# A two-pass plan for engine order, fixed places for early attention, and results staged in dead x rooms (block attention and relu-squared FFN, one core)

## The chip, the cores and the metric

The kernel runs on one core of one Trainium2 chip. Its time is the device time of one execution in microseconds (us); the median of three runs is 923.54 us (923.27 to 924.87). A profile is one more execution, recorded by the hardware. PE is the matrix engine (PEld its weight loads), DVE the vector engine, ACT the scalar engine, POOL the general one, SP the engine that mostly issues DMA transfers.

## The reference

Inputs: q, k, v of shape (8 batches, 8 heads, 576 positions, 64) in float32, and two weight matrices of float64, `w_in` (512 x 2048) and `w_out` (2048 x 512).

```
scores = q_c @ k_c^T / 8           # inside chunks of 64 positions
attn   = exp(scores - max); attn /= (sum(attn) + 1e-9)
x      = attn @ v_c                # heads side by side: (4608, 512)
h      = x @ w_in
out    = relu(h)**2 @ w_out        # (4608, 512)
```

## The kernel before

**Blocks.** The 4608 rows are 36 pairs of chunks (128 rows each), in nine blocks of four pairs. A block's FFN takes 16 steps, one for each 128 of the 2048 hidden columns. Step f multiplies a slab of `w_in` with the block's x (twelve matmuls, line L606 in `mm_in`, into tile h), applies relu (L617), square (L621 on DVE or L623 on ACT), and splits the result into a high and a low part (gh on L630, gl on L633). Two steps later (`LAG`) twelve matmuls on L643 (`mm_out`) add it to four accumulators o, one for each pair. Each product is three matmuls (high x high, high x low, low x high), since a single fp32r part does not hold float32. In a list of PE operations the three count as one entry.

**Results.** After step 15 each accumulator is copied out (`keep`, L651; even pairs on ACT, odd ones on DVE) into one of two slots of a tile called stage, and stored from there (`store`, L656). The accumulators' banks are those that the next block's first L643 matmuls write.

**Weights.** They arrive as float64 (`fetch_w`, L155 and L157, 512 KB a slab) in a tile called raw, viewed as 32-bit words: word 0 is the low one, word 1 the high one. `convert_w` makes an fp32 value of the bits and splits it: ups (L169, ACT) takes the rounding bits from word 0; sign (L173, DVE) writes the sign and top exponent bit as half words; size (L179, ACT) is the absolute value of word 1; clamp (L183, DVE) bounds it; shift (L188, DVE) moves it by three bits into tile a; up (L192, DVE) adds the two; high (L197, ACT) and low (L208, DVE) give the two parts in tile w. There are 32 slabs (items), ordered i0, i1, i2, o0, i3, o1 and so on (i of `w_in`, o of `w_out`). The first six are converted one by one (`SINGLE = 6`), the others two at a time. Tile a lies, for every other group, in the room that is later the stage tile.

**Attention of the first two blocks** (`Pair`, lines L494 to L582) is done in float32 by whole pairs: q and k turned on PE (L494), copied (L505, L509), scores (L518), maximum, difference, exponential, sum, reciprocal, product (L526 to L544), probabilities turned (L555, L561), values (L569), x placed as high and low part (`place`, L580 and L582). Pairs 0 to 3 lead; nothing of the FFN can start before their x. Pairs 4 to 7 run during block 0. The raw q and k of all eight lie in rooms that the last eight weight slabs take over, so these slabs are fetched only when a pair has been turned. v goes to vbd (L286), q and k to qk_raw (L250).

**Later attention** (`Unit`, half the heads of a pair at a time, lines L303 to L453) is spread through the FFN of the block before, at written places (`SPOTS`, and `LEAD` for the first). Its q and k come to three ring tiles (L278), for pair 8 first to the stage tile, and are transposed on DVE (L308). PE computes scores on L355, turns probabilities on L402 and computes values on L428; POOL does the product with 1/sum (L394), v's low part (L345) and x's low part (L453).

**Order.** `Plan.add` collects operations with an engine, an estimated cost, and tokens read and written. `Plan.run` simulates the engines once, from the start: always the operation that can start first, then the one with the earlier due time (or a rank given by hand). The order so found is the order in which instructions are issued to each engine; SP takes its early loads in the written order. Engines run their queues strictly in order.

Of the kernel before, what the change touches and what calls it, by code (L numbers as in the profile page):

```python
# [21 lines left out]
def kernel(  # L22
# [40 lines left out]
    SINGLE = 6  # L63
    XV = 4
    FROM = (8, 12, 16, 24)
    V_FROM = (8, 12, 16, 24)
    RANK = (8, 12, 16, 20)
    blocks = [4] * 9
    LAG = 2
    GBUFS = 2  # L70
# [88 lines left out]
    def convert_w(g):  # L159
# [8 lines left out]
        def ups():  # L168
            nc.scalar.activation(word(0).bitcast(I32), word(0), AF.Copy, scale=2.0 ** -29)  # L169

        def sign():
            half = rooms_of[g, "raw"].bitcast(U16)
            nc.vector.tensor_scalar(  # L173
                half[:, :, :, 1], half[:, :, :, 3], 0x8000, 0x4000, op0=ALU.bitwise_and, op1=ALU.bitwise_or
            )

        def size():
            a = word(1).bitcast(F32)
            nc.scalar.activation(a, a, AF.Abs)  # L179

        def clamp():
            a = word(1).bitcast(F32)
            nc.vector.tensor_scalar(a, a, EXP_MIN, EXP_MAX, op0=ALU.max, op1=ALU.min)  # L183

        def shift():
            pool, tag = (gp, "o") if g % 2 else (wst, "a")
            st["a"] = a = pool.tile([P, 2, DM], U32, name=f"a{g}", tag=tag, bufs=1)[:, :k]
            nc.vector.tensor_scalar(a, word(1), 3, 0xFFFFFFF8, op0=ALU.logical_shift_left, op1=ALU.bitwise_and)  # L188

        def up():  # L190
            c = st["a"].bitcast(I32)
            nc.vector.tensor_tensor(c, c, word(0).bitcast(I32), op=ALU.add)  # L192
# [19 lines left out]
        return ups, sign, size, clamp, shift, up, high, low  # L212
# [76 lines left out]
    class Unit:  # L289
# [155 lines left out]
        def place(self, part):  # L445

            xh, xl = x_of(self.b)
            dst = (slice(None), slice(self.hq * HP, (self.hq + 1) * HP), slice(self.j * P, (self.j + 1) * P))
            src = self.x.rearrange("p a c i -> p a (c i)")
            if part == 0:  # L450
                nc.scalar.copy(xh[dst], src)  # L451
            else:
                nc.gpsimd.tensor_tensor(xl[dst], src, xh.bitcast(F32)[dst], op=ALU.subtract)  # L453

    def x_of(b):
        if b not in xt:
            n = XB[b % 2]
            xt[b] = tuple(
                xp.tile([P, NCC, n * P], F32R, name=f"x{m}{b}", tag=f"x{m}{b % 2}") for m in "hl"
            )  # L460
        return xt[b]
# [16 lines left out]
    class Pair:  # L478
# [95 lines left out]
        def place(self, part):  # L574
            b = block_of[self.u]
            j = self.u - first_pair[b]
            ps = self.xt.rearrange("p a c i -> p a (c i)")
            xh, xl = (x[:, :, j * P:(j + 1) * P] for x in x_of(b))
            if part == 0:
                nc.scalar.copy(xh, ps)  # L580
            else:
                nc.vector.tensor_tensor(xl, ps, xh.bitcast(F32), op=ALU.subtract)  # L582
# [7 lines left out]
    class Step:  # L590
# [7 lines left out]
        def mm_in(self, c, i):  # L598
            if c == 0 and i == 0:
# [3 lines left out]
            xh, xl = xt[self.b]  # L603
# [3 lines left out]
                self.h[:, :self.n], a[:, c], bb[:, c, :self.n],  # L607
# [40 lines left out]
        def keep(self, j, n):  # L648
            o = stage(n)
            copy = nc.vector.tensor_copy if j % 2 else nc.scalar.copy  # L650
            copy(o, acc[self.b, j])  # L651
            kept[self.b, j] = o
# [10 lines left out]

    ffn = [Step(b, f) for b, f in steps]
# [5 lines left out]
    class Plan:  # L670
# [35 lines left out]
        def run(self):  # L706
# [20 lines left out]
            while open_:  # L727
# [17 lines left out]
                for x in after[n]:  # L745
                    ready[x] = max(ready[x], end + self.hop(n, x))
                    waits[x] -= 1
                    if not waits[x]:
                        open_.add(x)
            assert len(order) == len(ops)  # L750
# [6 lines left out]
    def program():  # L757
# [19 lines left out]
        def fetch(n):  # L777
            where = []
            for m in together[group_of[n]] if not place_in[n] else ():
                u = m - (n_items - NN)  # L780
                where += [("q", u), ("k", u)]
                if 2 <= u + XV < lead:
                    where.append(("v", u + XV))
            add(SP, ISSUE, lambda: fetch_w(n), writes=[("raw", n), *where], size=P * DM * 8)
# [18 lines left out]

        def turns(u):
# [3 lines left out]
            add(PE, 4 * 0.11, lambda: x.turn(0), [("q", u), "ident"], [bq])  # L808
# [3 lines left out]
            add(PE, 4 * 0.11, lambda: x.turn(1), [("k", u), "ident"], [bk])  # L812
            add(ACT, ONE, x.keep_k, [bk], [("kt", i)])

        def scores(u):
# [4 lines left out]
            add(PE, 16 * 0.11 + w, x.scores, [("qbd", i, 0), ("qbd", i, 1), ("kt", i)], [bs])  # L820
# [9 lines left out]

        def values(u):
            x = prs[u]
            i = u % 2
            bp, bx = x.banks["pt"], x.banks["xt"]
            tt = "g" if x.lead and i else "tt"
            if x.lead and u:
                p.rank = 0.9 + (u - 1) / 10
            add(PE, 4 * 0.11, x.turn_p, [("e", i), "ident"], [bp])
            add(ACT, ONE, x.keep_p, [bp], [tt])
            if x.lead and u:  # L840
                p.rank = 1 + u / 10
            add(PE, 16 * 0.11, x.values, [("v", slot_of(u)), tt], [bx])
            place(u)

        def attention(u):
            banks(u)
            for stage in (turns, scores, shares, values):
                stage(u)
# [17 lines left out]
        def place(u):  # L866
            x = prs[u]
            bx = x.banks["xt"]
            add(ACT, ONE, lambda: x.place(0), [bx], [("xh", u, hq) for hq in range(NQ)])
            add(DVE, TWO, lambda: x.place(1), [bx] + [("xh", u, hq) for hq in range(NQ)], [("xl", u, hq) for hq in range(NQ)])  # L870

        def convert(n):
# [4 lines left out]
            ups, sign, size, clamp, shift, up, high, low = convert_w(g)  # L877
            a = ["a"] if g % 2 == 0 else [("ob", 0), ("ob", 1)]
            raw = [("raw", n) for n in ns]
            half, two, one = (HALF, TWO, ONE) if len(ns) == 1 else (TWO, TWO + 0.53, ONE + 0.37)  # L880
# [319 lines left out]
```

## Time and profile before

| | us |
|---|---|
| median of 3 runs | 923.54 |
| the profiled execution | 923.09 |
| its span, first to last instruction | 921.3 |
| PE busy | 906.7 (98%) |
| DVE busy | 688.7 (75%) |
| ACT busy | 640.1 (69%) |
| POOL busy | 209.9 (23%) |
| mean granted PE clock | 0.999 of full speed |

Busy times are sums over the span. Matmuls overlap in PE's pipeline: a record's length is more than the distance to the next one, so a full row of PE says that it was never empty, not that it ran at its best. In rows of the timeline the columns are start, duration, engine, line, operation, output<-input, shapes, count; in brackets at the end, how long the engine idled before it and what ended that.

### The profile page before, as it was taken

Reading aid. Unit: us, or ns where it says so; the run is one execution under the profiler, and the core shown is the slowest. Engines: PE = TensorE matmul, PEld = TensorE weight load, DVE = VectorE, ACT = ScalarE, POOL = GpSimd, SP = SyncE. Lnnn points to the kernel's source line nnn. Section 1 sums busy time; section 2 is a strip of 40 time slices with the busy share of each in tenths; the row PEclk is TensorE's granted clock in tenths of the full one; section 3 lists DMA queues with packets and bytes.
Section 4 is the critical chain, followed back from the end, with each engine's and each line's share of the span. In section 5 each row is a group of like instructions: output and inputs, shape, how many; then the busy total and the mean of one; then the engine's idle time right before and its main releaser. Section 6 shows DMA issues by size and latency. Waiting matters only on the chain. (4 is left out here: it accounts for less than half of the span.)

```text
span 921.3 us, 14689 instructions
## 1 busy us (share of the span) xinstructions
PE 906.7 (98%) x4402; PEld 752.3 (82%) x4402; DVE 688.7 (75%) x1499; ACT 640.1 (69%) x1443; POOL 209.9 (23%) x351
## 2 busy tenths in 40 slices
PE   8999999999999999999999999999999999999997
PEld 7778888888778888888888888888888888888886
DVE  5989987889887778777888878777877787742111
ACT  5878877887777777777777777777777777743232
POOL 2000003333333323333222223322233333300000
PEclk9999999999999999999999999999999999999999
DMA  8889106222232223222232232223322231001001
GB/s 181 266 221 292 46 15 135 51 52 49 64 72 44 43 45 90 49 43 39 74 54 47 47 81 50 44 47 67 72 45 43 43 90 36 1 1 47 0 1 46
DMA packets 222671, 62.85 MB, mean 68 GB/s; under 512 B 207744, under 2 KB 215936, under 8 KB 222592
## 3 DMA queue, kind: packets, MB, share of 16 engines
q1 hardware_dynamic: 220480, 61.39, 28.9%
q10 hardware_dynamic: 2112, 0.52, 0.3%
q8 instruction: 36, 0.59, 0.3%
q14 instruction: 43, 0.35, 0.1%
HBM read 52.43 MB, written 9.44 MB: 67 GB/s over the span
## 5 line engine op out<-in xcount | busy, mean ns | idle before, releaser
L606 PE MATMUL h<-xh,w 128*128 128x512 f32 x1152 | 402.4, 396 | 1.1 <-DVE w L208 0.7
L643 PE MATMUL o<-w,gh 128*128 128x512 f32 x1152 | 359.0, 393 | 2.7 <-DVE stage L651 2.4
L606 PEld LDWEIGHTS h<-xh,w 128*128 128x128 f32 x1152 | 216.1, 188 | 45.0 <-DVE w L208 3.0
L643 PEld LDWEIGHTS o<-w,gh 128*128 128x128 f32 x1152 | 211.3, 188 | 47.7 <-DVE stage L651 5.8
L606 PE MATMUL h<-xl,w 128*128 128x512 f32 x576 | 225.2, 391 | 0.4 <-POOL xl L453 0.4
L643 PE MATMUL o<-w,gl 128*128 128x512 f32 x576 | 224.3, 389 | 0.0
L633 DVE TENSOR_TENSOR gl<-g,gh 128x512 fp32r<-128x512 f32 x144 | 103.3, 718 | 106.5 <-ACT gh L630 99.8
L617 ACT ACTIVATE g<-h 128x512 f32<-128x512 f32 x144 | 86.0, 597 | 86.1 <-PE h L606 72.8
L345 POOL TENSOR_TENSOR vs<-v_raw,vs 64x128 fp32r<-64x128 f32 x224 | 125.6, 561 | 33.5 <-ACT vs L340 21.7
L643 PEld LDWEIGHTS o<-w,gl 128*128 128x128 f32 x576 | 108.2, 188 | 23.3
L606 PEld LDWEIGHTS h<-xl,w 128*128 128x128 f32 x576 | 108.7, 189 | 19.2 <-POOL xl L453 0.8
L630 ACT CAST gh<-g 128x512 fp32r<-128x512 f32 x144 | 89.3, 620 | 43.7 <-PE o L643 37.9
L394 POOL TENSOR_TENSOR e<-e,z 128x256 f32<-128x256 f32 x56 | 36.6, 654 | 286.4 <-DVE z L391 189.9
L368 ACT COPY e<-sc 64x128 f32<-64x128 f32 x224 | 58.0, 259 | 45.3 <-PE sc L355 42.6
L373 DVE TENSOR_TENSOR e<-sc,e 64x128 f32<-64x128 f32 x224 | 64.6, 288 | 27.2 <-ACT e L368 23.2
L453 POOL TENSOR_TENSOR xl<-x,xh 128x256 fp32r<-128x256 f32 x56 | 41.4, 740 | 160.9 <-ACT xh L451 152.7
L443 DVE TENSOR_TENSOR x<-xt,x 64x128 f32<-64x128 f32 x224 | 64.6, 288 | 11.1 <-ACT x L438 5.6
L325 ACT CAST kst<-ring 64x512 fp32r<-64x512 f32 x112 | 69.0, 616 | 3.0 <-DVE ring L308 1.2
L438 ACT COPY x<-xt 64x128 f32<-64x128 f32 x224 | 58.1, 260 | 17.4 <-PE xt L428 12.1
L621 DVE TENSOR_TENSOR g<-g 128x512 f32<-128x512 f32 x64 | 48.6, 760 | 28.8 <-ACT g L617 28.1
L417 DVE TENSOR_TENSOR pst<-pt,pst 64x256 fp32r<-64x256 f32 x112 | 47.2, 422 | 12.1 <-ACT pst L413 10.0
L623 ACT ACTIVATE g<-g 128x512 f32<-128x512 f32 x80 | 50.6, 632 | 2.3
(71 smaller groups left out, 917.6 us busy)
## 6 DMA issues: line engine op xcount, KB each, us to landing
v_raw<-in_v_dram SPq DMA_DIRECT2D x112, 128.0 KB, 3.2
out_dram<-stage SPq DMA_DIRECT2D x36, 256.0 KB, 2.1
raw<-in_moe_w_in_dram SPq DMA_DIRECT2D x16, 512.0 KB, 6.2
raw<-in_moe_w_out_dram SPq DMA_DIRECT2D x16, 512.0 KB, 7.1
ring<-in_q_dram SPq DMA_DIRECT2D x216, 32.0 KB, 2.1
ring<-in_k_dram SPq DMA_DIRECT2D x216, 32.0 KB, 2.0
vbd<-in_v_dram SPq DMA_DIRECT2D x32, 64.0 KB, 2.9
qk_raw<-in_q_dram SPq DMA_DIRECT2D x14, 128.0 KB, 4.9
```

The costliest lines, as they stand in the source:

```text
L325: nc.scalar.copy(late["k"][other[c][half], 0, c], pairs[self.pair]["t", 1][own])
L345: nc.gpsimd.tensor_tensor(self.v[:, c][dst], self.raw_v(c)[dst], self.v.bitcast(F32)[:, c][dst], op=ALU.subtract)
L368: nc.scalar.copy(self.e[r, 2 * part:2 * part + 2], self.done[part][r, :, 1, c])
L373: nc.vector.tensor_tensor(e, self.done[part][r, :, 0, c], e, op=ALU.add)
L438: nc.scalar.copy(self.x[r, hp], self.xt[hp][r, :, 1, h2])
L443: nc.vector.tensor_tensor(x, self.xt[hp][r, :, 0, h2], x, op=ALU.add)
L606: nc.tensor.matmul(self.h[:, :self.n], a[:, c], bb[:, c, :self.n], start=c == 0 and i == 0, stop=c == NCC - 1 and i == 2,)
L617: nc.scalar.activation(self.g, self.h[:, :self.n], AF.Relu)
L623: nc.scalar.activation(self.g, self.g, AF.Square)
L630: nc.scalar.copy(self.gh[:, :self.n], self.g)
L633: nc.vector.tensor_tensor(self.gl[:, :self.n], self.g, self.gh.bitcast(F32)[:, :self.n], op=ALU.subtract)
L643: nc.tensor.matmul(acc[b, j], a[:, j * P:(j + 1) * P], bb, start=f == 0 and i == 0, stop=f == NF - 1 and i == 2,)
```

## The change

- **Plan in two passes.** The old simulation stays as a first order (`greedy`). Then, up to six times (`ROUNDS`), every operation is moved as late as it can go, from the last to the first (`to_the_right`), and then as early as it can go, in order of these latest times (`to_the_left`), filling gaps on its engine and on the DMA queue. The plan with the earliest end on PE is used.
- **First block's attention at fixed places.** Pairs 4 to 7 are no longer ranked against conversions: their four stages (turns; scores; probabilities turned; values) stand at `EARLY = (0, 0.25, 0.55, 0.75)` of a quarter of block 0's operation list, and all of these and the FFN's operations form one fixed order on PE. The last four slabs are fetched and converted behind the turns of pairs 5 and 7. The plan counts a slab's transfer at 0.6 of its size.
- **Loads.** The first two slabs are issued before the v loads of pairs 1 to 3; loads of pairs 4 to 7 follow the lead, with their order left to the plan.
- **Conversions.** All groups have two slabs (`SINGLE = 0`). size writes tile a, clamp and shift work in place there, sign works on the whole word 1, and ups writes its bits into the lower half of that word. There are still eight instructions.
- **x in halves.** A block's x is two tiles for high and two for low part, by half of the heads, and the first two blocks place them with two instructions each in place of one.
- **Results.** `keep` writes to a tile in the room of the finished block's second x half (pairs 0 and 1 in xh's, 2 and 3 in xl's), four slots in place of two; the very last pair's copy is cut into halves on ACT and DVE. The x of two blocks later waits for these stores.
- `LEAD` goes from 0.105 to 0.08.

```
-    SINGLE = 6
+    SINGLE = 0
+    EARLY = (0.0, 0.25, 0.55, 0.75)
...
+        def size():
             pool, tag = (gp, "o") if g % 2 else (wst, "a")
             st["a"] = a = pool.tile([P, 2, DM], U32, name=f"a{g}", tag=tag, bufs=1)[:, :k]
+            nc.scalar.activation(a.bitcast(F32), word(1).bitcast(F32), AF.Abs)
...
+        def sign():
+            a = word(1)
+            nc.vector.tensor_scalar(a, a, 0x80000000, 0x40000000, op0=ALU.bitwise_and, op1=ALU.bitwise_or)
+        def ups():
+            half = rooms_of[g, "raw"].bitcast(U16)
+            nc.scalar.activation(half[:, :, :, 2], word(0), AF.Copy, scale=2.0 ** -29)
...
-        def keep(self, j, n):
-            o = stage(n)
-            copy = nc.vector.tensor_copy if j % 2 else nc.scalar.copy
-            copy(o, acc[self.b, j])
-            kept[self.b, j] = o
+        def keep(self, j, cols):
+            if (self.b, j) not in kept:
+                m = "hl"[j // HP]
+                if (m, self.b) not in result:
+                    tag = f"x{m}{NQ - 1}{self.b % 2}"
+                    result[m, self.b] = xp.tile([P, HP, DM], F32, name=f"out{m}{self.b}", tag=tag)
+                kept[self.b, j] = result[m, self.b][:, j % HP]
+            copy = nc.vector.tensor_copy if j % 2 ^ (cols is HALF_ONE) else nc.scalar.copy
+            copy(kept[self.b, j][:, cols], acc[self.b, j][:, cols])
...
+        def to_the_right(self, start, after):
+            ops = self.ops
+            last = max(start[n] + ops[n][1] for n in start)
+            busy = self.busy()
+            right = {}
+            for n in sorted(start, key=lambda n: (start[n], n), reverse=True):
+                engine, cost, _, _, size, _ = ops[n]
+                t = min((right[x] - self.hop(n, x) for x in after[n]), default=last)
+                if size:
+                    t = self.lately(busy, "queue", t - self.LATENCY, size / self.RATE)
+                right[n] = self.lately(busy, engine, t, cost)
+            return right
+        def to_the_left(self, right):
+            ops = self.ops
+            busy = self.busy()
+            start, end = {}, {}
+            for n in sorted(right, key=lambda n: (right[n], n)):
+                engine, cost, _, before, size, _ = ops[n]
+                t = max((end[x] + self.hop(x, n) for x in before), default=0.0)
+                start[n] = t = self.early(busy, engine, t, cost)
+                end[n] = t + cost
+                if size:
+                    end[n] = self.early(busy, "queue", t + cost, size / self.RATE) + size / self.RATE + self.LATENCY
+            return start
...
+            start = self.greedy()
+            end = lambda start: max(start[n] + op[1] for n, op in enumerate(ops) if op[0] == PE)
+            best = start
+            for _ in range(ROUNDS):
+                start = self.to_the_left(self.to_the_right(start, after))
+                if end(start) < end(best):
+                    best = start
...
+        load_values(0)
+        for n in range(2):
+            fetch(n)
+        for u in range(1, lead):
+            load_values(u)
+        leading()
+        p.rank = None
+        for u in range(lead, NN):
+            load(u)
+        for u in range(lead, lead + 2):
+            load_values(u)
+        for n in range(2, n_items - NN + lead):
+            fetch(n)
...
+        spots = [
+            ((i + x) / lead, [lambda u=lead + i, n=n: at_spot(u, n)]) for i in range(lead) for n, x in enumerate(EARLY)
+        ]
+        spread(ops, spots)
...
-    LEAD = 0.105
+    LEAD = 0.08
...
+            old = [[("out", un.b % 2, HP * m + j) for j in range(HP)] if (un.j, un.hq) == (0, NQ - 1) else [] for m in range(2)]
+            add(ACT, 0.42, lambda: un.place(0), x, [("xh", i, un.hq), *old[0]])
+            add(POOL, 0.85, lambda: un.place(1), [*x, ("xh", i, un.hq)], [("xl", i, un.hq), *old[1]])
```

More of the change, by code (lines that the diff above doesn't have):

```diff
@@ L1 @@
+import bisect
 import itertools
@@ L210, in low @@
             )
-        return ups, sign, size, clamp, shift, up, high, low
+        return size, clamp, shift, sign, ups, up, high, low
     units = []
@@ L749, in run, with busy, early @@
                         open_.add(x)
+            return {n: t for t, n in order}
+        def busy(self):
+            return {e: ([], []) for e in (*self.HOP, "queue")}
+        def early(self, busy, resource, t, cost):
+            starts, ends = busy[resource]
+            i = bisect.bisect_right(ends, t)
+            while i < len(starts) and starts[i] < t + cost - 1e-9:
+                t = max(t, ends[i])
+                i += 1
+            starts.insert(i, t)
+            ends.insert(i, t + cost)
+            return t
@@ new lines, in run @@
+        def run(self):
+            ops = self.ops
+            after = [[] for _ in ops]
+            for n, op in enumerate(ops):
+                for x in op[3]:
+                    after[x].append(n)
+            start = self.greedy()
[5 more added lines that the diff above has]
+                    best = start
+            order = [(t, n) for n, t in best.items()]
+            due = [0] * len(ops)
@@ L829, in shares, with weights_of, pe_chain @@
             add(DVE, TWO, x.norm, [("z", i)], [("e", i)])
+        def weights_of(u):
+            x = prs[u]
+            i = u % 2
+            tt = "g" if x.lead and i else "tt"
+            bp = x.banks["pt"]
+            if x.lead and u:
+                p.rank = 0.9 + (u - 1) / 10
+            add(PE, 4 * 0.11, x.turn_p, [("e", i), "ident"], [bp] + pe_chain(x))
+            add(ACT, ONE, x.keep_p, [bp], [tt])
+        def pe_chain(x):
+            return [] if x.lead else ["pe"]
         def values(u):
@@ L833, in values @@
             i = u % 2
-            bp, bx = x.banks["pt"], x.banks["xt"]
+            bx = x.banks["xt"]
             tt = "g" if x.lead and i else "tt"
[L836 to L839, printed above, removed]
+            if x.lead:
+                weights_of(u)
             if x.lead and u:
                 p.rank = 1 + u / 10
-            add(PE, 16 * 0.11, x.values, [("v", slot_of(u)), tt], [bx])
+            add(PE, 16 * 0.11, x.values, [("v", slot_of(u)), *used("v", u), tt], [bx] + pe_chain(x))
             place(u)
[L845 to L848, printed above, removed]
         def leading():
@@ L868, in place @@
             bx = x.banks["xt"]
[L869 to L870 removed]
+            for hq in range(NQ):
+                add(ACT, 0.42, lambda hq=hq: x.place(0, hq), [bx], [("xh", u, hq)])
+            for hq in range(NQ):
+                add(DVE, 0.42, lambda hq=hq: x.place(1, hq), [bx, ("xh", u, hq)], [("xl", u, hq)])
         def convert(n):
@@ L876, in convert @@
                 return
-            ups, sign, size, clamp, shift, up, high, low = convert_w(g)
+            size, clamp, shift, sign, ups, up, high, low = convert_w(g)
             a = ["a"] if g % 2 == 0 else [("ob", 0), ("ob", 1)]
             raw = [("raw", n) for n in ns]
-            half, two, one = (HALF, TWO, ONE) if len(ns) == 1 else (TWO, TWO + 0.53, ONE + 0.37)
-            add(ACT, one + 0.06, ups, raw, [("up", g)])
-            add(DVE, half, sign, [*raw, ("up", g)], [("sign", g)])
-            add(ACT, one + 0.06, size, [("sign", g)], raw)
-            add(DVE, half, clamp, [], raw)
-            add(DVE, half, shift, raw, a)
-            add(DVE, two, up, [*raw, ("sign", g)], a)
+            half, two, one = (HALF, TWO, ONE) if len(ns) == 1 else (HALF + 0.2, TWO + 0.38, ONE + 0.37)
+            add(ACT, one + 0.06, size, raw, a)
+            add(DVE, half, sign, [], raw)
+            add(DVE, half, clamp, [], a)
+            add(DVE, half, shift, [], a)
+            add(ACT, one + 0.06, ups, [], raw)
+            add(DVE, two, up, raw, a)
             add(ACT, one, high, a, [*raw, *(("wh", n) for n in ns)])
```

163 lines of the change are left out of this document (83 added, 80 removed).

## The prediction

> **What bounds the kernel now.** The page comes first: is one engine full from end to end?
>
> ```profile
> span 921.3 us, 14689 instructions
> PE 906.7 (98%) x4402; PEld 752.3 (82%) x4402; DVE 688.7 (75%) x1499; ACT 640.1 (69%) x1443; POOL 209.9 (23%) x351
> ```
>
> PE is. The FFN work cannot shrink, so all that can be won is what PE does not run at its pace, and what lies before its first and after its last FFN matmul. The chain that ended last gives the pace:
>
> ```profile
> 823.44 2.72 PE h L606 x12
> 826.16 2.72 PE o L643 x12
> ...
> 837.04 2.98 PE o L643 x12
> ```
>
> Twelve matmuls take 2.72, 0.227 each, 0.68 for a group of three. The third row is 0.26 over: a stop. Next come busy times by block of the FFN (columns: stretch, its length, then busy time of PE, PEld, DVE, ACT, POOL, the clock, DMA share, GB/s). The stretches are cut at the first matmul of each block's step 0.
>
> ```profile
> 29.73:75.00 45.27, 43.16 (x221) 33.74 (x221) 41.77 (x64) 37.05 (x56) 0.00 (x0) 1.00 0.85 250
> 75.00:134.30 59.30, 59.30 (x306) 49.53 (x305) 55.82 (x68) 48.34 (x64) 0.00 (x0) 1.00 0.32 94
> 134.30:237.40 103.10, 101.98 (x482) 83.88 (x481) 88.69 (x205) 78.96 (x193) 33.98 (x55) 1.00 0.35 69
> 237.40:336.30 98.90, 97.59 (x466) 80.95 (x465) 79.31 (x188) 74.30 (x184) 29.41 (x50) 1.00 0.27 55
> 336.30:433.80 97.50, 97.31 (x466) 81.02 (x465) 78.53 (x186) 72.57 (x179) 28.70 (x49) 1.00 0.27 55
> ```
>
> PE idles 2.11 early in block 0, nothing in its second part, 1.12 in block 1, 1.31 in block 2, 0.19 in a later block. A matmul's record lasts 0.39, 0.16 longer than its pace, so each stop hides up to 0.16 beyond the idle shown. With some eight stops, block 0 loses 2.1 to 3.4; I take 3.4, so its pure work is 104.57 - 3.4 = 101.2. In that block DVE is busy 41.77 + 55.82 = 97.59 of 104.57, 93%: it is what stops PE there.
>
> **The change, part by part.**
>
> *Results in dead x rooms, planned order.* Every block's end shows the same stop:
>
> ```profile
> 738.68 0.36 SPq L656 DMA_DIRECT2D out_dram<-stage  x1
> ...
> 743.50 0.69 DVE L651 COPY stage<-o 128x512 f32<-128x512 f32 x1
> ...
> 744.25 0.72 PE L643 MATMUL o<-w,gh 128*128 128x512 f32 x2 [0.19 <-DVE stage L651]
> ...
> 153.85 0.50 PE L643 MATMUL o<-w,gh 128*128 128x512 f32 x1 [0.52 <-DVE stage L651]
> ...
> 256.75 0.73 PE L643 MATMUL o<-w,gh 128*128 128x512 f32 x2 [0.94 <-DVE stage L651]
> ```
>
> With two stage slots, copy j = 3 needs store j = 1 (issued at 738.68) landed, so its place in DVE's order is late (743.50), and PE, which must reuse that bank, stops. With four rooms per block it can follow PE's last group directly. With the hidden 0.16: five blocks x 0.35, then 0.68, 1.10 and the 0.26 of 837.04, together 3.8. What could be late next: the copies still share DVE with 78 us of work per 97.5, so I credit 3.3 (bounds 0, if the new order leaves the copy last, and 3.8). The new waits: the first write of the reused rooms (xh on ACT, xl on POOL, pair 0, second half of the heads) waits for the stores of the block before. It comes about a fifth of a block, 19 us, in. The last outputs end two steps in, 16 groups of 0.68 and some attention, about 12; copy 0.7 and store 2.9 (as at the end, below) make 15.6. Behind that wait on POOL stand v splits and norms; with 3 us of slack, zero.
>
> *The end.*
>
> ```profile
> 915.82 0.39 PE L643 MATMUL o<-w,gl 128*128 128x512 f32 x1
> ...
> 916.94 0.58 ACT L651 COPY stage<-o 128x512 f32<-128x512 f32 x1 [2.15 <-DMA out_dram<-stage]
> 917.75 0.69 DVE L651 COPY stage<-o 128x512 f32<-128x512 f32 x1 [2.18 <-DMA out_dram<-stage]
> ```
>
> Both last copies wait for stores. The final copy ends at 918.44, 2.86 before the span ends (its store). Without the wait, j = 3 starts after PE's end (916.21) and a hop of 0.05; as two halves on two engines it takes about 0.42 (an estimate, between half of 0.69 and 0.69): 916.68. Gain 918.44 - 916.68 = 1.75 (bounds 1.4 for an unsplit copy, 1.85).
>
> *Conversions: pairs throughout, whole-word sign, contiguous clamp.* The groups of instructions up to 125 us, by shape:
>
> ```profile
> L173 DVE TENSOR_SCALAR raw<-raw 128x1024 uint16<-128x1024 uint16 x12 | 16.1, 1340 | 0.0
> L192 DVE CUSTOM_DVE_ANT_0 a<-raw,a 128x2048 uint16<-128x2048 uint16 x11 | 13.5, 1225 | 0.3
> L179 ACT ACTIVATE raw<-raw 128x1024 f32<-128x1024 f32 x11 | 12.6, 1144 | 2.3 <-DVE raw L173 2.3
> L208 DVE TENSOR_TENSOR w<-a,w 128x1024 fp32r<-128x1024 f32 x10 | 12.4, 1235 | 2.8 <-ACT w L197 2.8
> L197 ACT CAST w<-a 128x1024 fp32r<-128x1024 f32 x11 | 11.6, 1051 | 6.3 <-DVE a L192 6.3
> ...
> L188 DVE TENSOR_SCALAR a<-raw 128x1024 uint32<-128x1024 uint32 x11 | 7.6, 694 | 0.3
> L183 DVE TENSOR_SCALAR raw<-raw 128x1024 f32<-128x1024 f32 x11 | 7.6, 691 | 1.3 <-ACT raw L179 1.2
> ...
> L582 DVE TENSOR_TENSOR xl<-xt,xh 128x512 fp32r<-128x512 f32 x8 | 5.4, 686 | 0.0
> ...
> L173 DVE TENSOR_SCALAR raw<-raw 128x512 uint16<-128x512 uint16 x6 | 4.2, 771 | 0.0
> ```
>
> The old sign (L173) works on half words, 1.340 for a pair of slabs. On whole words it is the same bitwise kind and stride as the shift (L188, 0.694) and the in-place stride of the clamp (L183, 0.691): I take 0.69, with 1.34 as upper bound. Thirteen pairs save 13 x 0.65 = 8.4 of DVE time, six singles about 6 x (0.77 - 0.35) = 2.5. Halving the x placement costs at most 0.69 more for each of four pairs inside this stretch, 2.7. So DVE in block 0 falls from 97.6 to about 89.4. That is no gain by itself; it takes DVE's share from 93% to 85% and so removes the cause of the stops. I leave 1.0 of 3.4: gain 2.4 (bounds 0 and 3.4).
>
> The Trainium skill, "VectorE: DVE Perf Modes", section "What auto-detection actually checks", has every one-source operation between SBUF operands with an even outer dimension run at two results a cycle. By that the old sign would already run at the rate of the clamp and the edit would bring DVE nothing; the trace disagrees, with 1340 ns against 691 ns for the same 1024 elements, and the trace decides.
>
> *First block's attention at fixed places, loads reordered.* Pair 4's q and k transposes stand at place 0, so PE now takes them ahead of the first FFN matmul; today they come 13 us behind it.
>
> ```profile
> 15.00:17.50 2.50, 2.21 (x21) 1.98 (x19) 1.70 (x4) 2.14 (x4) 0.00 (x0) 1.00 0.56 118
> ...
> 19.15 2.57 SPq L286 DMA_DIRECT2D vbd<-in_v_dram  x4
> 25.26 3.13 SPq L250 DMA_DIRECT2D qk_raw<-in_q_dram  x4
> 29.36 5.87 SPq L250 DMA_DIRECT2D qk_raw<-in_k_dram  x4
> ...
> vbd<-in_v_dram SPq DMA_DIRECT2D x4, 64.0 KB, 3.8
> ...
> 28.58 0.58 ACT L580 CAST xh<-xt 128x512 fp32r<-128x512 f32 x1
> ...
> 29.73 0.50 PE L606 MATMUL h<-xh,w 128*128 128x512 f32 x1 [0.32 <-ACT w L197]
> ...
> 43.41 0.60 PE L494 MATMUL k<-ident,qk_raw 128*128 128x128 f32 x4
> ```
>
> Around 15 us the DMA engines are half idle (share 0.56): SP's issuing is the limit, 0.64 for each 64 KB piece. Moving two weight slabs ahead of three v loads fills that hole and starts conversion 0 some 3 to 5 us sooner; the number of issues up to the last lead v stays, so it still ends at 21.72. Pair 4 crosses a batch, so q and k are eight pieces: 8 x 0.64 = 5.1, to 26.9; landing 3.8 (the row of the last lead v) and transposing 0.60 give 31.3. If slabs 2 and 3 slip between, 1.1 more. I take 31.4: 1.7 later than 29.73. Bounds: 29.0, when loads for pair 4 go early and x itself (28.58 plus a half copy) decides; 39.6, if they stay where they are (35.23 + 3.8 + 0.6). The delay lets conversions run ahead, which is one more reason for the clean block 0.
>
> Block 1's first late scores move from 0.105 to 0.08 of the block, 15 to 11 groups of 0.68 in. They need q and k of pair 8, whose loads use the room that a conversion holds:
>
> ```profile
> 132.56 3.78 SPq L278 DMA_DIRECT2D stage<-in_q_dram  x8
> ...
> 136.73 1.23 DVE L208 TENSOR_TENSOR w<-a,w 128x1024 fp32r<-128x1024 f32 x1 [1.12 <-ACT w L197]
> ...
> 147.22 0.64 PE L355 MATMUL sc<-kst,qst 128*128 128x256 f32 x4
> ```
>
> Load to scores takes 147.22 - 132.56 = 14.7. Block 1 now starts at 31.4 + 101.2 + 1.0 = 133.6, its scores at 133.6 + 11 x 0.68 = 141.1, so the loads must start by 126.4. The room now belongs to the last group, fetched once pair 7 is transposed at three quarters of block 0, 31.4 + 0.75 x 101.2 = 107.3. Its chain is size 1.14, clamp 0.69, shift 0.69, up 1.23, high 1.05, low 1.24, together 6.0, which leaves 13.1 for loading and queueing. I take no stop. The other stops in blocks 1 and 2 (1.12 - 0.52 + 1.31 - 0.94 = 1.0 shown, up to 1.9 with the hidden part) hang on single orders of DVE, ACT and POOL; a plan from both ends may clear half: 1.0 gained (bounds 0 and 1.9).
>
> **Sum.** +1.7 - 2.4 - 1.0 - 3.3 - 1.75 = -6.75. The profiled execution took 923.09 (1.8 beside its span); 916.3, and 0.45 more against the median of 923.54: 916.8.
>
> **The rivals.**
>
> *Everything comes off:* start at 29.0 (-0.7), 3.4, 1.9, 3.8 and 1.75 gained: -11.6, on the median 911.9. For it: half-idle DMA before 20 us. Against: DVE still over 80% busy in every block with attention.
>
> *Pair 4's loads stay late:* PE starts FFN at 39.6 (+9.9), block 0 is then clean (-3.4), the rest as forecast: -3.4 - 1.0 - 3.3 - 1.75 + 9.9 = +0.45, 924.0, no measurable change. For it: six slabs stand ahead of them in SP's order today. Against: the order is now by latest times, which knows that PE needs them first.
>
> *The last conversion is late:* if its low ends where it does now, 137.96, the first late scores stand at 137.96 + 14.7 = 152.7 instead of 141.1, and PE, whose order is fixed, stops 11.5: 928.3, slower. It decides once that low ends after 126.4 + 6.75 = 133.2. For it: DVE is 94% busy from 75 to 134 (55.82 of 59.30), and the last group can only be fetched late. Against: the lighter DVE and the 13.1 of slack.
>
> *The sign edit does nothing:* whole words in place run at 1.34 as well. DVE then stays above 95% in block 0, its 3.4 of stops remain: 916.8 + 2.4 = 919.2. For it stands the skill's equal rate for both forms; against it rows L183 and L188.
>
> **How the numbers follow.** Forecast 0.62, everything comes off 0.15, sign edit nothing 0.07, loads late 0.07, last conversion late 0.09. About 0.2% (1.85) is what a measurement of this kernel can tell from no change. The first three are faster, 0.84; loads late is the same, 0.07; last conversion late is slower, 0.09. The range runs from the best case to half the forecast's gain given back at the start or at the late scores: 911.9 to 921.5, leaving out the two bad cases.
>
> **What would show it.** Right: PE's first h matmul between 29 and 33 behind two groups of L494; sign rows near 0.69; no PE idle released by L651; last copies right behind PE's last matmul, 1.75 less from there to the end; block 0 with less than 1 us of idle. Wrong: an idle stretch of PE ahead of pair 4's transposes or of the first four L355 matmuls; DVE copies of results still following gl; a stop somewhere in blocks 3 to 8 that the old order did not have.

## The result, and the profile after

The changed kernel takes 932.23 us (median of 4 runs, 930.71 to 932.51) against 923.55 for the kernel before on the same chip: ratio 1.0088, 95% interval 1.0070 to 1.0105. It is slower, by 8.7 us of the medians; the forecast was 6.75 faster. The profiled execution took 930.71. One execution of `e1_ups_word` below, 1290.57 us at a granted clock of 0.654, is left out of its median. The page of the changed kernel:

```profile
span 928.9 us, 14638 instructions
PE 908.8 (98%) x4402; PEld 758.0 (82%) x4402; DVE 684.4 (74%) x1492; ACT 661.8 (71%) x1443; POOL 219.1 (24%) x351
```

DVE is 4.3 less busy than before, as meant. ACT is 21.7 busier, which nothing in the forecast had. The busy times by block of the FFN, cut at the first h matmul of each block (columns as in the table of the prediction):

```profile
32.00:148.30 116.30, 107.70 (x528) 88.55 (x529) 89.79 (x124) 104.83 (x120) 2.00 (x3) 0.96 0.52 156
148.30:250.70 102.40, 98.80 (x470) 81.73 (x470) 85.80 (x202) 76.94 (x190) 31.35 (x53) 1.00 0.33 65
250.70:347.70 97.00, 97.00 (x466) 81.10 (x465) 81.23 (x188) 73.73 (x181) 30.66 (x49) 1.00 0.27 55
347.70:444.70 97.00, 97.00 (x466) 81.10 (x465) 79.46 (x186) 73.20 (x179) 30.63 (x49) 1.00 0.27 55
```

From block 2 on PE never idles: 97.0 a block where there were 98.9 and 97.5. All the loss lies before block 2, most of it in block 0. Block 0 takes 116.30; before, counted to the same matmul, it took 107.3 (104.57, and the 2.72 of twelve L643 matmuls that stood behind the cut):

```profile
29.73:137.02 107.29, 105.18 (x536) 85.53 (x537) 99.16 (x133) 86.76 (x121) 0.00 (x0) 1.00 0.54 159
```

In block 0 PE now idles 8.6 (116.30 - 107.70), before 2.1. ACT is busy 104.83, or 90%, and the granted PE clock is 0.96. What ACT does there, by shape (window 0 to 150 us), and below it the same instruction in the kernel before (window 0 to 125):

```profile
L187 ACT ACTIVATE raw<-raw 128x1024 uint16<-128x1024 uint32 x16 | 40.3, 2521 | 0.8 <-DVE raw L183 0.8
L171 ACT ACTIVATE a<-raw 128x1024 f32<-128x1024 f32 x16 | 18.5, 1157 | 4.4 <-DMA raw<-in_moe_w_out_dram 2.4 <-DMA raw<-in_moe_w_in_dram 1.7 <-DVE w L207 0.3
```

```profile
L169 ACT ACTIVATE raw<-raw 128x1024 int32<-128x1024 uint32 x12 | 13.9, 1157 | 0.0
```

`ups` reads the same 1024 words and makes the same values, but writes them as two-byte numbers 8 bytes apart, and takes 2.521 instead of 1.157: for the 16 groups 16 x 1.364 = 21.8 us more on ACT, all of it before the end of block 0. The DVE side of a conversion came out as forecast (`sign` L183 0.689, `clamp` L175 0.686, `shift` L179 0.691):

```profile
L191 DVE CUSTOM_DVE_ANT_0 a<-raw,a 128x2048 uint16<-128x2048 uint16 x16 | 19.6, 1225 | 11.4 <-ACT raw L187 10.8
...
L183 DVE TENSOR_SCALAR raw<-raw 128x1024 uint32<-128x1024 uint32 x16 | 11.0, 689 | 3.0 <-ACT a L171 2.9
```

The first row's last column is the new wait: ahead of the 16 `up`, DVE sat idle 10.8 us in all for `ups`. What queues behind `up` on DVE and ACT is the attention of the next pair, and PE has that at a fixed place. PE at the turns of pair 5's and of pair 6's probabilities, and DVE ahead of the second, from the timeline:

```profile
80.86 0.63 PE L553 MATMUL pt<-ident,ne 128*128 128x128 f32 x4 [2.52 <-DVE ne L542]
...
102.60 1.23 DVE L191 CUSTOM_DVE_ANT_0 a<-raw,a 128x2048 uint16<-128x2048 uint16 x1 [1.74 <-ACT raw L187]
...
106.21 0.39 PE L641 MATMUL o<-w,gl 128*128 128x512 f32 x1
...
108.22 0.69 DVE L542 TENSOR_TENSOR ne<-ne,nz 128x512 f32<-128x512 f32 x1
...
109.05 0.63 PE L553 MATMUL pt<-ident,ne 128*128 128x128 f32 x4 [2.45 <-DVE ne L542]
109.44 1.01 PE L641 MATMUL o<-w,gh 128*128 128x512 f32 x2
...
110.68 1.05 PE L641 MATMUL o<-w,gh 128*128 128x512 f32 x2
```

These are two stops of 2.5. Ahead of the second, DVE waits 1.74 for `ups` before `up`, and two more instructions of the conversions stand between it and the pair's maximum in DVE's order, and one more behind that. After it, a group of three matmuls takes 1.24 (109.44 to 110.68), not 0.68. The clock column (0.50, 0.54) of two stretches shows why:

```profile
42.00:48.20 6.20, 5.98 (x14) 4.37 (x15) 4.67 (x7) 5.77 (x6) 0.00 (x0) 0.50 1.11 333
...
109.40:112.80 3.40, 3.40 (x11) 2.64 (x10) 3.40 (x5) 3.12 (x7) 0.00 (x0) 0.54 0.00 0
```

PE is "busy" almost throughout, at a granted clock of 0.50 and 0.54: the matmuls run at half pace. By the clock records the half pace lasts 6.8 us, from 41.4, and 3.4 us, from 109.7; ten us at half pace can cost up to 5. The second stretch follows the stop of 2.45; the first follows one of 1.09 and sixteen narrow matmuls (scores, 39.74 to 41.93). The stop of 2.52 that ends at 80.86 had no such stretch. The Trainium skill, "TensorE: Matmul & The Clock Gate", Part 1 (the HAM clock gate), has the clock halved after at least one idle window of about 3.4 us, and the window runs freely. The lengths of 3.4 and 6.8 agree with a window of that size; that a whole idle window is needed does not, since 2.45 was enough here, and the measurement decides.

Block 1 then loses 2.0. Its first late scores, whose loads wait for the room of the last conversion, stop PE for 1.59; two stops of 1.07 and 0.91 follow (166.20, 169.85, behind POOL's product and DVE's low part of the probabilities), where the kernel before had 1.12 in all:

```profile
143.91 2.31 SPq L277 DMA_DIRECT2D stage<-in_q_dram  x5
...
157.58 0.71 PE L354 MATMUL sc<-kst,qst 128*128 128x256 f32 x4 [1.59 <-ACT kst L324]
```

The start and the end, from the timeline:

```profile
29.25 0.61 PE L492 MATMUL q<-ident,qk_raw 128*128 128x128 f32 x4
30.38 0.63 PE L492 MATMUL k<-ident,qk_raw 128*128 128x128 f32 x4 [0.51 <-PE q L492]
...
31.99 0.50 PE L604 MATMUL h<-xh,w 128*128 128x512 f32 x1
...
924.24 1.05 ACT L654 COPY outl<-o 128x512 f32<-128x512 f32 x2 [0.72 <-PE o L641]
...
924.49 0.39 PE L641 MATMUL o<-w,gl 128*128 128x512 f32 x1
...
925.32 0.42 DVE L654 COPY outl<-o 128x256 f32<-128x256 f32 x1 [1.00 <-ACT outl L654]
```

FFN begins at 32.0 behind pair 4's turns. After the last matmul's start there are 928.9 - 924.49 = 4.4 us, before 5.5.

So the 7.6 us of span (921.3 to 928.9) split up as: start +2.3, block 0 +9.0, block 1 +2.0 (102.4 against 134.30 + 2.72 to 237.40, 100.4), block 2 -1.9, blocks 3 to 7 -2.5, end -1.1, block 8 -0.3 (each rounded by itself).

### The profile page after: what moved, and what is told of

The parts are those of the page before. It is cut to its first block, busy times and chain, and to the rows that moved or that the text cites. A ratio compares the mean times of both kernels' runs of the same rounds, so it can differ in the third digit from the quotient of the medians.

```text
span 928.9 us, 14638 instructions
## 1 busy us (share of the span) xinstructions
PE 908.8 (98%) x4402; PEld 758.0 (82%) x4402; DVE 684.4 (74%) x1492; ACT 661.8 (71%) x1443; POOL 219.1 (24%) x351
## 4 chain that ended last, share of the span: by engine, by line
PE 81%; issue 0%; DVE 0%; ACT 0%
PE o L641 37%; PE h L604 37%; PE xt L427 3%; PE sc L354 3%; PE pt L401 1%; DVE pst L416 0%; DVE outl L654 0%; ACT outl L654 0%
## 5 line engine op out<-in xcount | busy, mean ns | idle before, releaser
L344 POOL TENSOR_TENSOR vs<-v_raw,vs 64x128 fp32r<-64x128 f32 x224 | 128.2, 572 | 78.1 <-ACT vs L339 68.0
L631 DVE TENSOR_TENSOR gl<-g,gh 128x512 fp32r<-128x512 f32 x144 | 101.1, 702 | 55.7 <-ACT gh L628 52.7
L453 POOL TENSOR_TENSOR xl<-x,xh 128x256 fp32r<-128x256 f32 x56 | 48.7, 870 | 163.5 <-ACT xh L450 157.8
```

What stands on the lines that cost most here:

```text
L344: nc.gpsimd.tensor_tensor(self.v[:, c][dst], self.raw_v(c)[dst], self.v.bitcast(F32)[:, c][dst], op=ALU.subtract)
L631: nc.vector.tensor_tensor(self.gl[:, :self.n], self.g, self.gh.bitcast(F32)[:, :self.n], op=ALU.subtract)
```

## The experiments

Theory A: the two-byte write of `ups` makes ACT the engine that block 0 waits for. Rivals: the fixed places, the two-pass plan, or the earlier late scores by themselves. All kernels, with the end of the last conversion's `low` and the start of block 2 from the traces (us); the ratio is to the kernel before on the same chip:

| kernel | ups | last low ends | block 2 starts | span | median | ratio, 95% |
|---|---|---|---|---|---|---|
| before | 1.16 | 137.96 | 237.4 | 921.3 | 923.55 | 1 |
| after | 2.52 | 143.88 | 250.7 | 928.9 | 932.23 | 1.0070-1.0105 |
| e1_ups_word | 1.16 | 131.17 | 237.9 | 915.9 | 917.59 | 0.9917-0.9947 |
| e2_ups16_before | 2.55 | 145.75 | 245.3 | 929.2 | 930.89 | 1.0069-1.0101 |
| e3_rooms_before | 1.16 | 136.67 | 238.8 | 917.7 | 919.19 | 0.9943-0.9968 |
| e4_no_fixed | 2.52 | 150.27 | 255.7 | 933.7 | 937.65 | 1.0137-1.0168 |
| e5_old_words | 1.15 | 132.94 | 238.7 | 916.7 | 920.48 | 0.9946-0.9971 |
| e6_pool_ups | 4.68 | 165.54 | 273.0 | 952.0 | 954.51 | 1.0314-1.0342 |
| e7_one_pass | 1.16 | 127.95 | 237.6 | 915.6 | 917.27 | 0.9912-0.9939 |
| e9_near_halves | 1.39 | 131.40 | 237.4 | 915.3 | 918.62 | 0.9936-0.9962 |
| e10_near_one_pass | 1.38 | 136.52 | 244.7 | 922.7 | 923.95 | 0.9992-1.0009 |
| e12_conversions_before | 1.38 | 139.49 | 244.7 | 929.9 | 930.38 | 1.0055-1.0082 |
| e13_one_pass_after | 2.5 | 141.57 | 250.9 | 928.9 | 930.90 | 1.0070-1.0098 |
| e14_one_pass_told | 2.5 | 143.82 | 250.8 | 928.7 | 930.62 | 1.0060-1.0085 |

**The write by itself: out of the new kernel, into the old one.**

```
# e1: after, one line
-            nc.scalar.activation(half[:, :, :, 2], word(0), AF.Copy, scale=2.0 ** -29)
+            nc.scalar.activation(word(0).bitcast(I32), word(0), AF.Copy, scale=2.0 ** -29)
# e2: before, the same line the other way
-            nc.scalar.activation(word(0).bitcast(I32), word(0), AF.Copy, scale=2.0 ** -29)
+            half = rooms_of[g, "raw"].bitcast(U16)
+            nc.scalar.activation(half[:, :, :, 0], word(0), AF.Copy, scale=2.0 ** -29)
```

> The changed kernel, but ups writes whole 32-bit words to word 0, as before the change; the rounding bits are then not added (up still adds word 1), so the last three bits of each weight are left out. Nothing else moves: same order, same waits. Theory A (two-byte writes on ACT cost 2.52 us in place of 1.16, and so ACT becomes the bound of block 0): ups near 1.16, ACT in block 0 from 104.8 busy down by 16 x 1.36 = 22, the stops ahead of turning the probabilities (1.3, 2.7 and 2.6 us) and the half-clock stretches behind them gone, time 917 to 921. Theory B (the fixed places of early attention in PE's order make stops of any lateness): the stops stay, 926 to 931. Theory C (the two-pass order is bad for DVE in block 0): as B.

> The kernel before, with one edit: ups writes its bits as two-byte values into the lower half of word 0 (the upper half is written by sign anyway, so the result is the same). Theory A: ups from 1.16 to about 2.5 for pairs and from 0.69 to about 1.3 for singles, 13 x 1.36 + 6 x 0.6 = 21 more on ACT, whose busy time in block 0 was 85 of 105; block 0 becomes ACT-bound and 5 to 11 us longer: 929 to 935. Theories B and C: the width of the write is harmless, 923 to 925.

Each way the write alone carries the loss: without it the change takes 917.59 (the rounding bits are then left out; order and waits stay), with it the kernel before goes to 930.89. e1 keeps the fixed places, the two-pass plan and the earlier late scores, so none of these makes the loss by itself. Block 0 of e1:

```profile
31.90:137.50 105.60, 103.72 (x531) 86.78 (x529) 89.65 (x124) 87.01 (x120) 1.99 (x3) 0.98 0.59 175
```

It has the same DVE time as after (89.8), 17.8 less on ACT, and 10.7 less of block. PE still idles 1.89 in it (105.60 - 103.72), little less than the 2.1 of before.

**Result rooms alone, in the old kernel** (the x halves, the four rooms and the split last copy; old plan, old conversions).

```
-            xt[b] = tuple(xp.tile([P, NCC, n * P], F32R, name=f"x{m}{b}", ...) for m in "hl")
+            xt[m, b, hq] = xp.tile([P, HP, XB[b % 2] * P], F32R, name=name, tag=name[:-1] + str(b % 2))
...
-                    ob = ("ob", next(stores) % 2)
+                    ob = ("out", s.b % 2, j)
```

> The kernel before with only the result rooms: x in halves by heads, results copied to the dead second halves (four slots), the last copy cut into halves, old one-pass plan. The prediction's terms: stops at the seven block ends gone (3.8) and the end 1.1 to 1.75 shorter: 917.5 to 920. Rival (the old plan leaves the copies late in DVE's order all the same): only the end is shorter, 922 to 922.8.

919.19, as expected. From the start of block 2 to the end of the span it takes 917.7 - 238.8 = 678.9, where before takes 683.9 and after 678.2: 5.0 of the 5.7 that the changed kernel gains there are the rooms and the split copy.

**Without the fixed places.** In `pe_chain`, `return [] if x.lead else ["pe"]` becomes `return []`.

> The changed kernel without the token that ties early attention into one fixed PE order with the FFN; the plan places these groups itself, everything else stays, two-byte ups included. Theory A: ACT stays the bound of block 0, 928 to 933. Theory B: PE runs FFN matmuls where it now stops, 920 to 925. Theory C: as A.

937.65, above its range of 928 to 933. The fixed places are not the loss; without them it is larger, with stops of 4.60 ahead of the first FFN matmul (34.26), 5.29 ahead of a pair's scores (83.09) and 5.67 ahead of the first late scores (163.24).

**Old words under the new plan** (after, with `ups` to word 0 as int32 and `sign` on half words, both as before; nothing left out).

```
-            nc.vector.tensor_scalar(a, a, 0x80000000, 0x40000000, op0=ALU.bitwise_and, op1=ALU.bitwise_or)
+            nc.vector.tensor_scalar(half[:, :, :, 1], half[:, :, :, 3], 0x8000, 0x4000, op0=..., op1=...)
...
-            nc.scalar.activation(half[:, :, :, 2], word(0), AF.Copy, scale=2.0 ** -29)
+            nc.scalar.activation(word(0).bitcast(I32), word(0), AF.Copy, scale=2.0 ** -29)
```

> The changed kernel with the old handling of words alone: ups writes 32-bit words to word 0, sign half words over their upper half, up adds word 0; nothing is left out. Theory A: ACT as in e1, but sign 1.34 in place of 0.69 puts 16 x 0.65 = 10.4 back on DVE (its plan cost raised to match). If DVE's room in block 0 matters as the prediction held (93% busy makes stops): 919 to 922. If it does not: 917 to 918.5, as e1.

920.48 (the profiled execution took 918.48), inside the range that was to mean that DVE's room matters. Its block 0 says otherwise:

```profile
34.90:137.20 102.30, 102.30 (x531) 86.93 (x530) 94.49 (x122) 84.42 (x117) 2.00 (x3) 0.99 0.55 160
```

DVE is 92% busy (94.49 of 102.30), `sign` takes 1.335, and PE does not idle once. What the kernel loses against e1 it loses before: block 0 starts at 34.9, 3.0 later, because a k of pair 4 landed late (PE waited 3.3 for it), and is 3.3 shorter. Whether the late start, in which conversions run ahead, is what makes the block clean is not separated here.

**The write on POOL.** `nc.gpsimd.tensor_scalar(half[:, :, :, 2], word(0), 2.0 ** -29, None, op0=ALU.mult)`.

> The changed kernel with ups, two-byte write and all, moved from ACT to POOL, which is idle in block 0; planned at 2.5 us; nothing is left out. Theory A: ACT loses 16 x 2.52 in block 0 and the stops go, 914.5 to 918, below e1's 917.6 if block 0 gets cleaner still. Against: POOL's own time for 1024 two-byte elements, unknown here (its nearest row is 0.74 for 256 elements, so some 3 us), or its sharing something with DVE, stretches the chain of a conversion: 919 to 925.

954.51, far above both ranges. One `ups` takes 4.675, and DVE's own instructions grow (window 0 to 150):

```profile
L187 POOL TENSOR_SCALAR raw<-raw 128x1024 uint16<-128x1024 uint32 x15 | 70.1, 4675 | 70.1 <-DVE raw L183 46.7 <-DMA qk_raw<-in_q_dram 20.0 <-DMA vbd<-in_v_dram 3.3
```

```profile
L207 DVE TENSOR_TENSOR w<-a,w 128x1024 fp32r<-128x1024 f32 x15 | 26.4, 1759 | 2.7 <-ACT w L196 2.7
L179 DVE TENSOR_SCALAR a<-a 128x1024 uint32<-128x1024 uint32 x15 | 21.6, 1443 | 0.2
L175 DVE TENSOR_SCALAR a<-a 128x1024 f32<-128x1024 f32 x15 | 20.7, 1381 | 0.0
L191 DVE CUSTOM_DVE_ANT_0 a<-raw,a 128x2048 uint16<-128x2048 uint16 x15 | 18.3, 1220 | 4.9 <-POOL raw L187 3.6
```

**One pass instead of two,** e1 with `ROUNDS = 0`.

> e1 (whole-word ups, rounding bits left out) with the first, forward plan alone (no rounds of the two passes). Theory C (the two passes are bad for block 0): 916 or less. Otherwise the two passes are worth what they clear in blocks 1 and 2 beyond e3's result rooms: 918.5 to 922.

917.27 against 917.59, between its two ranges: with these conversions the two passes are worth nothing.

**What makes the write slow.** Extra ACT instructions behind the last late attention of e1, two of each form.

> e1 with ten extra ACT instructions on dead tiles in the last block, 512 elements each, two of each form, to price the write by itself: (1) two-byte elements 8 bytes apart, in place; (2) two-byte, next to each other; (3) two-byte, 4 bytes apart; (4) 32-bit, next to each other; (5) 32-bit, 8 bytes apart. Theory A as width: 1, 2 and 3 near 1.37, 4 and 5 near 0.69. As partly written words: 1 and 3 near 1.37, 2 near 0.69. As distance: only 1 slow.

> The changed kernel with ups as an int32 write to word 0 (the rounding bits are left out) and twelve extra ACT instructions behind its last late attention, six forms twice each: two-byte integer 8 bytes apart into another tile, 512 elements; 16 bytes apart, 256; 8 bytes apart, 256; 4 bytes apart into another tile, 512; 4 bytes apart in place, 512; bfloat16 8 bytes apart into another tile, 512. If distance is the cause: about 1.37, .7 or more, .7, .78, .78 and 1.37. If working in place is the cause: .67 to .78 for the first three and the sixth, with only the in-place form slow. If the integer type is the cause: the sixth at .67. Total time 917 to 922, of no interest.

Mean durations in e8 and then e11 (late window, by shape; the first row of e8 mixes contiguous at 0.67 and 4 bytes apart at 0.78; ring is contiguous for the int32 row, stage is 8 bytes apart):

```profile
L1241 ACT ACTIVATE ring<-stage 128x512 uint16<-128x512 uint32 x4 | 2.9, 724 | 0.0
L1241 ACT ACTIVATE stage<-stage 128x512 uint16<-128x512 uint32 x2 | 2.7, 1362 | 0.0
...
L1241 ACT ACTIVATE stage<-stage 128x512 int32<-128x512 uint32 x2 | 1.4, 681 | 0.0
L1241 ACT ACTIVATE ring<-stage 128x512 int32<-128x512 uint32 x2 | 1.3, 666 | 0.0
```

```profile
L1243 ACT ACTIVATE ring<-ring 128x512 uint16<-128x512 uint32 x4 | 3.1, 784 | 0.0
L1243 ACT ACTIVATE stage<-ring 128x512 uint16<-128x512 uint32 x2 | 2.7, 1358 | 0.0
L1243 ACT ACTIVATE stage<-ring 128x512 bf16<-128x512 uint32 x2 | 2.7, 1353 | 0.0
```

```profile
800.58 1.36 ACT L1243 ACTIVATE stage<-ring 128x256 uint16<-128x256 uint32 x1
...
805.96 0.77 ACT L1243 ACTIVATE stage<-ring 128x256 uint16<-128x256 uint32 x1
```

The last two are 256 elements 16 and 8 bytes apart. The cause is neither working in place nor the integer type; the time goes by the stretch that the two-byte results span. 2048 bytes (256 x 8, 512 x 4) take 0.77 to 0.78, 4096 bytes (256 x 16, 512 x 8) 1.36, so 0.29 us for each KB over some 0.18; for 1024 x 8 that makes an estimate of 2.5, and `ups` has 2.52. Below 2 KB the line does not hold: 512 contiguous elements, 1 KB, take 0.67. Four-byte results over the same 4096 bytes take 0.68. The Trainium skill, "SBUF — State Buffer", section "Door 1: The DMA port swizzle", has lines of 16 bytes and full rate as long as each is hit at least twice, so that a stride of 8 bytes should be free for both types; the int32 row agrees, the two-byte row (1.36 against 0.67 contiguous) does not, and the measurement decides.

**A version that avoids it.** `sign` writes tile a, `ups` writes into a's lower halves (4 bytes apart), `size`, `clamp` and `shift` work in place on word 1; nothing is left out.

```
+            nc.vector.tensor_scalar(a, word(1), 0x80000000, 0x40000000, op0=..., op1=...)     # sign
+            half = st["a"].bitcast(U16).rearrange("p k (n w) -> p k n w", w=2)
+            nc.scalar.activation(half[:, :, :, 0], word(0), AF.Copy, scale=2.0 ** -29)        # ups
```

> The changed kernel with its conversions rearranged and nothing left out: sign writes whole words to the contiguous tile a, ups writes its two-byte results into the lower halves of a (4 bytes apart instead of 8), size, clamp and shift work in place on word 1. Theory A, refined by the probes (a two-byte ACT write is slow at a distance of 8 bytes, not at 4): ups takes some 1.45 for 1024 elements, ACT in block 0 falls from 104.8 by 16 x 1.1 to about 88, the early stops mostly go: 916 to 918.5, ratio .992 to .995. Rival, that any two-byte ACT write of this size is slow: ups stays at 2.5 and the time at 930 to 932. Rival, that the two-pass plan is what lengthens block 0: over 925 with ups at 1.45.

> The same kernel with the plan of one pass (no moving late and early afterwards). If the two passes matter once conversions fit, it is over 1 us slower than the two-pass version; if, as with the int32 write, they are worth nothing beyond the chip's scatter, it is within 1 us: 916 to 918.5.

e9 takes 918.62, just over its range in time and inside it in ratio, 0.9949 (0.9936 to 0.9962): faster than both kernels, with the rest of the change in it. By shape and by block:

```profile
L187 ACT ACTIVATE a<-raw 128x1024 uint16<-128x1024 uint32 x16 | 22.2, 1386 | 0.0
```

```profile
33.80:135.80 102.00, 102.00 (x530) 86.81 (x529) 86.61 (x120) 85.24 (x116) 2.00 (x3) 0.99 0.56 165
135.80:237.40 101.60, 98.77 (x470) 81.68 (x469) 85.56 (x202) 77.63 (x191) 31.47 (x53) 1.00 0.33 66
```

Block 0 is without a stop. With one pass the same conversions give 923.95, 5.3 slower: there DVE's queue held `sign` of the second group, whose slab landed late, ahead of `up` of the first, and FFN began at 38.4:

```profile
34.31 0.69 DVE L183 TENSOR_SCALAR a<-raw 128x1024 uint32<-128x1024 uint32 x1 [4.54 <-DMA raw<-in_moe_w_out_dram]
...
38.36 0.79 PE L604 MATMUL h<-xh,w 128*128 128x512 f32 x1 [6.36 <-ACT w L196]
```

So the two passes are worth 5 in one arrangement and nothing in another: they mend an order that the first plan happens to get wrong.

**Lighter conversions in the old plan:** `before` with e9's conversions.

> The kernel before with only its conversions rearranged as in the first kernel of this call (whole-word sign; two-byte ups 4 bytes apart; nothing left out), the first six still one by one, old plan, old result rooms. It tests the term of the prediction for block 0 alone: if room on DVE takes away the stops there, as forecast, 920 to 922 (2.4 of 3.4 gained). If the stops hang on the order of the old plan or on the longer chain of a conversion, 923 to 925.

930.38, above both ranges. Block 0, then PE at a stop and the stretch behind it:

```profile
30.64:143.79 113.15, 107.04 (x536) 88.89 (x537) 91.75 (x134) 92.80 (x126) 2.00 (x3) 0.97 0.54 155
...
79.00:86.00 7.00, 6.32 (x27) 5.74 (x26) 4.19 (x6) 2.70 (x5) 0.00 (x0) 0.54 0.37 68
```

```profile
78.57 0.63 PE L555 MATMUL pt<-ident,ne 128*128 128x128 f32 x4 [1.84 <-DVE ne L544]
```

DVE has 7.4 less to do than before and is at 81%, and PE idles 6.1 (113.15 - 107.04), where it idled 2.1 with DVE at 92%. The new conversions also change the order of work on DVE and ACT and put 3.7 more on ACT for `ups`, so e12 does not tell which of these makes the stops.

**Wrong estimate, or too much work?** The plan costs `ups` at 1.2. e13 is after with one pass, e14 the same with one number changed: `add(ACT, 2.46, ups, [], raw)`.

> The changed kernel with the plan of one pass (ROUNDS = 0), nothing else changed. ups still takes 2.5 us. If the two-byte write alone lengthens block 0, the loss is about the same: 928 to 936. If the two passes themselves make the loss, 922 to 925.

> The same one-pass plan, with ups costed at 2.46 in the plan, near what the trace shows, instead of the old 1.2. If the loss comes from the plan believing a duration that is wrong (work placed on ACT that is late on the chip), the plan that knows better gets back more than half of the loss: below 925. If it comes from the work itself, ACT being full in block 0, it stays within 3 us of the kernel that believes the old duration.

930.90 and 930.62: telling the plan changes nothing in the time. e13 also answers the rival of the two-pass plan, since with one pass the loss is as large. Blocks 0 and 1 of e13, then of e14:

```profile
31.70:149.40 117.70, 104.79 (x529) 86.65 (x530) 90.09 (x125) 105.45 (x121) 1.99 (x3) 0.99 0.53 155
149.40:250.90 101.50, 99.19 (x470) 81.58 (x469) 85.47 (x202) 77.72 (x190) 32.08 (x52) 1.00 0.34 67
```

```profile
31.70:144.20 112.50, 105.56 (x529) 86.28 (x530) 89.22 (x124) 104.94 (x121) 2.00 (x3) 0.98 0.53 159
144.20:250.80 106.60, 100.48 (x470) 82.80 (x469) 86.19 (x203) 78.45 (x190) 31.97 (x52) 0.98 0.34 67
```

The better estimate does take 5.2 out of block 0, and block 1 gives 5.1 back, with one stop of 5.0 at the first late scores. Its last conversion ends no earlier (143.82 against 141.57). With 105 us of ACT work in block 0, neither of the two orders ends it sooner; in the kernels with new conversions and new order block 2 starts 105 to 110 us after it. The two-pass plan with the true duration wasn't run, so what it would have made of it is open.

## Why the prediction was wrong, point by point

- **The step that failed** is the part on conversions. It priced every DVE instruction of a conversion from rows, and the chain of the last group as "size 1.14, clamp 0.69, shift 0.69, up 1.23, high 1.05, low 1.24", without `ups`. An ACT instruction whose output had become two-byte and strided was thereby costed at its old 1.157, that is, at nothing. The trace of before had no row for that form. It should have been bounded; `sign` on half words, 1.340 against 0.69 in the prediction's own table, was the nearest row, and a factor of two on 16 x 1.157 is 18.5. The runs showed 2.521: +21.8 on ACT, where block 0 had 37.05 + 48.34 = 85.4 of 104.57 in use and so 19.2 free. That one term carries the miss: taking it out moves the changed kernel from 1.0088 of the kernel before to 0.9932 (e1), putting it into the old one moves that to 1.0085 (e2).
- **Start:** 31.4 forecast, 32.0 measured, pair 4's turns ahead as described. In e9 (33.8) and e5 (34.9) the rival of late loads shows in small.
- **Block 0's stops (-2.4):** right in the sum with the start, but not for the reason given, which is luck. Once `ups` is short, PE comes to block 1 at 135.8 (e9) to 137.5 (e1), against 137.0 before: start and block together give +0.5 to -1.2, forecast -0.7. The forecast had DVE's share stop PE. But PE does not stop at 92% in e5 and stops more at 81% in e12, and e1, with the light DVE that was forecast (85%), idles 1.89, almost as before. The two kernels without a stop, e9 and e5, start block 0 late (33.8, 34.9); those that start at 31.9 and 32.4, e1 and e7, idle 1.89 and 2.81. What makes the block clean, the order on PE or the conversions that run ahead during a late start, stays open. The forecast also moved pair 4's turns (1.2) ahead of block 0 without taking them out of its 101.2.
- **Stops of blocks 1 and 2 (-1.0):** wrong in block 1. Block 2 is 1.9 shorter, 1.0 of it its block end by e3 (98.9 to 97.9). Block 1 is 0.1 (e1), 1.2 (e9) and 2.0 (after) longer although its block end is gone. In after and e9 the first late scores wait for their loads (1.59, 0.94), for which the forecast had 13.1 to spare; in all three two stops of about 1 behind POOL's product and DVE's low part of the probabilities remain. No run changes `LEAD` alone, so how much of it the earlier late scores make is not shown.
- **Block ends (-3.3):** right: 2.5 in blocks 3 to 7 (0.5 each, forecast 0.35), 1.0 in block 2, and PE idle nowhere in the rows of these blocks.
- **End (-1.75):** 1.1, in e1 and e9 1.4, the lower bound. In the changed kernel DVE's half starts at 925.32, 0.44 after PE's end (924.88) and not 0.05, released by ACT's half; the copy then ends 0.86 after PE instead of 2.23, and 0.3 more goes from there to the end of the span.
- **The rival "last conversion is late"** has the right chain: scores 13.7 after the end of the last `low`, forecast 14.7, and that end is at 143.88, past the 133.2 from which it was to decide. Its cause was unforeseen, and its price in block 1 was small (1.59 of idle), with block 0 itself 9.0 longer.
- **"The sign edit does nothing":** the row came out at 0.689, so the rival fell. What the edit is worth in time is not settled: e5 with the old sign and e9 with the new one have overlapping intervals, while e1, which beside the sign and its place in the plan differs from e5 only in the rounding bits left out, is 0.26% faster, with intervals that just meet.
- The forecast's sum, 916.3 for a profiled execution, is near what the change gives without the failed step: e9's took 917.45, e1's 917.69. Term by term it is not: e9 has +4.1 at the start and -5.3 in block 0 where +1.7 and -2.4 stood. And the upper bound of the range, 921.5, is not half of the gain given back, which makes 920.2.

## What to carry to other kernels

Price every instruction whose output type or stride changes, on every engine, also when its count and its element count stay: bound it by the nearest strided row. When a block's engine shares are 80 to 93%, read the free time on each engine (here 19 us on ACT) and ask which edit adds to it. DVE's share did not predict PE's stops here (none at 92%, many at 81%); how much ACT had to do did, as e1 and e2 show.

## What the runs showed of the hardware

- A two-byte ACT write costs by the stretch it spans: 0.77 to 0.78 for 2 KB, 1.36 for 4 KB, 2.52 for 8 KB, about 0.29 us a KB. Four-byte writes over the same stretch do not (0.68 for 4 KB, 1.16 for 8 KB).
- A short stop of PE can be followed by 3.4 or 6.8 us at half clock: after 2.45 at 109.05 here and after 1.84 in e12 it was, so that a stop can cost twice its length or more; after 2.52 at 80.86 it was not.
- A two-byte strided write of 1024 elements on POOL takes 4.68. In that kernel DVE's `clamp` and `shift` go from 0.69 to 1.38 and 1.44 and `low` from 1.22 to 1.76, while ACT's instructions keep their times (`size` 1.14). The eleven `low` that ran wholly beside a POOL write took 1.95 in the mean, the four that ran apart 1.22. `up` stays at 1.22, but 15 of the 16 ran while POOL wrote nothing, so its row says nothing either way. The Trainium skill, "Advanced Engine Details and Errata", section "Mode Summary", has VectorE's second port shared with GPSIMD, so that VectorE instructions in a two-port mode and GPSIMD's hold each other up; the rows of `clamp` and `shift` agree, and `low`, which has two sources, slows as well.
